# Shifting the SBUF buffers of a banded-attention and MoE kernel against each other by a few dozen bytes

## The chip, the cores and the metric

The kernel runs on one core of one Trainium2 chip. The metric is the device time of one execution in microseconds; the median of three runs of the kernel before is 660.24 us (659.09 to 661.42).

## The reference

Attention over 2 batches, 8 heads, 768 positions and 64 dimensions, in which each position sees its neighbours within 16 positions and, beside them, 24 summaries of blocks of 32 (the maximum of k, the mean of v). Two feed-forward stages follow on 1536 tokens of width 512:

```python
def _attn_ref(q, k, v):
    k_sum = k.reshape(B, H, nb, block, D).max(axis=3)
    v_sum = v.reshape(B, H, nb, block, D).mean(axis=3)
    scores_l = scale * np.matmul(q, k.transpose(0, 1, 3, 2))
    mask_l = np.abs(pos[:, None] - pos[None, :]) < window
    scores_s = scale * np.einsum('bhsd,bhnd->bhsn', q, k_sum) + np.log(block)
    a = softmax(concat([where(mask_l, scores_l, -1e9), scores_s]))
    return a @ concat([v, v_sum], axis=2)

def _moe_ref(x, w_a, w_b, w_out):        # 512 -> 1536 -> 512
    return ((x @ w_a) * (x @ w_b)) @ w_out

def _moe2_ref(x, w_in, w_out):           # 512 -> 2048 -> 512
    h = x @ w_in
    return (h - np.tanh(h)) @ w_out
```

## The kernel before

All matrices are held in float32. For the products of the two MoE stages each operand is split into a high and a low part of type fp32r, and three matmuls stand for one product: high by high, high by low, low by high. The tokens are handled in three blocks of 512, the hidden width in pieces of 128: 12 pieces in the first stage, 16 in the second.

The matmuls of these stages have 128 rows and columns of stationary weights and a moving operand of 512 columns, and stand on three lines:

- `proj` (line 370), called by `pos_a`, `pos_b` and `pos_h`: stationary a slice of the split weights `wsp`, moving a slice of the split tokens `X`, which lie in buffer `XA` or `XB`. Twelve matmuls make one PSUM tile (`pa`, `pb`, and in the second stage also `ps`, `pt`).
- `pos_o` (line 398): stationary `wsp`, moving `gh` or `gl`, the split gated hidden piece. Twelve matmuls, three into each of four `acc` tiles.
- `pos_o2` (line 459): stationary a slice of `gh` or `gl`, or, for every third piece, of two buffers of `vw`; moving the split weights `wsp`. Twelve matmuls into four `acc` tiles.

`wsp` has four buffers of 4096 bytes of each partition; one is filled for each piece of weights, by ACT (line 184, high part) and DVE or POOL (line 185, low part). Weights arrive as raw words by DMA in `stage`, `x21a` and `x21b` and are decoded by ACT, POOL and DVE into `w`.

The order of the work is a table: the list `pos` holds the steps of the two MoE stages, and a plan hangs the attention of the second batch (`T1`, `T2`, `T2b`, `T3`, `T4`) and the decoding of weights on its places, so that attention fills the first 300 us between the products of the first stage. The attention of the first batch stands ahead of it, as a list of operations by hand (`SEQ`). Attention's products are plain fp32: `T2m` (line 288; scores; moving `kw`, in steps of 480 bytes, stationary `qbd`, in steps of 512), transposes against `ident` (lines 223, 269, 327), `T4` (line 340), and the mean of v in `mean_v` (line 240; stationary `mavg` of 24 columns). A plain fp32 product has two records in the trace, an fp32r product or a transpose one.

Every buffer is a tile of one pool, `sb`, made by `st(shape, tag, bufs)`. The pool gives each tag its bytes in the order in which the tags are first asked for; the sizes that were asked for earlier decide where a later one lies. Nothing but such a size separates two neighbours. In the kernel before, one tile that nothing uses, `pad1` (128 bytes of each partition, line 780), follows `kt` (12672 bytes, 128 more than a multiple of 256).

Of the kernel before, what the change touches and what calls it, by code (L numbers as in the profile page):

```python
# [39 lines left out]
def band_attention_moe_kernel(ctx: ExitStack, tc: tile.TileContext, q, k, v, w_a, w_b, w_out, w_in, w_out2, out):  # L40
# [22 lines left out]
    def st(shape, tag, bufs=1, dt=F32):  # L63
        return sb.tile(shape, dt, tag=tag, bufs=bufs, name=tag)

    def pt(tag, shape=(128, 512)):
        return ps.tile(list(shape), F32, tag=tag, name=tag)
# [8 lines left out]
    qbd = st([128, 2, NP, 128], "qbd")  # L76
    qbd2 = st([128, 2, NP, 128], "wsp", 4)

    xb = st([128, 2 * KC * TB], "XB")
    kq = xb[:, 0:3072].rearrange("p (c h d) -> p c h d", c=NC, h=H)  # L80
    qbd4 = st([128, 2, NP, 128], "wsp", 4)
# [2 lines left out]
    def constants():  # L84
        nc.vector.memset(bsq, -math.sqrt(GA) * GB)
        nc.vector.memset(bth, -GC2)
        nc.vector.memset(qbd2, 0.0)
        nc.gpsimd.memset(qbd3, 0.0)

        for m, n, r in ((mavp, KW + 2 * NB - 8, BLK // 2), (mavg, 2 * NB - 4, BLK)):  # L90
            nc.gpsimd.memset(m, 1.0 / BLK)
            nc.gpsimd.affine_select(
                out=m, in_=m, pattern=[[-r, n]], compare_op=ALU.is_gt, fill=0.0,
                base=(n - NB) * r + 1, channel_multiplier=1,
            )
            nc.gpsimd.affine_select(
                out=m, in_=m, pattern=[[r, n]], compare_op=ALU.is_gt, fill=0.0,
                base=r - (n - NB) * r, channel_multiplier=-1,
            )
        nc.gpsimd.memset(qbd4, 0.0)  # L100
        for m, off in zip(masks, (0, WIN, 2 * WIN)):
            nc.gpsimd.memset(m[:, 0:KW], 0.0)
            nc.gpsimd.memset(m[:, KW:NK], math.log(BLK) / SC)
            for h in range(2):
                band = m[h * 64 : h * 64 + 64, 0:KW]
                nc.gpsimd.affine_select(
                    out=band, in_=band, pattern=[[1, KW]], compare_op=ALU.is_gt, fill=NEG,
                    base=WIN - off, channel_multiplier=-1,
                )
                nc.gpsimd.affine_select(  # L110
                    out=band, in_=band, pattern=[[-1, KW]], compare_op=ALU.is_gt, fill=NEG,
                    base=WIN + off, channel_multiplier=1,
                )
# [76 lines left out]
    kt, knat, qn, vst, qb, at_x, X = {}, {}, {}, {}, {}, {}, {}  # L190
    kwb = [st([128, NP, NK], "kw", 2) for _ in range(2)]
    kwb += [st([128, NP, NK], "w", 3 * F1) for _ in range(2)]
    vwb = [st([NK, H, D], "vw", 3) for _ in range(3)]
    vwx = [st([NK, H, D], "w", 3 * F1) for _ in range(5)]
    kwx = {}
    qx = {}
# [576 lines left out]
    with tc.manual_schedule():  # L773
        nc.vector.memset(qbd, 0.0)
        for _ in range(WARM):
            mm(pt("ps")[:, 0:256], qbd[:, 0, 0, :], qbd[:, 0, 0:2, :], start=True, stop=True)
        make_identity(nc, ident)
        XAv = st([128, 4, 2 * TB], "XA")
        kt[0] = st([128, NP, S + NB], "kt")
        st([128, 32], "pad1")  # L780
        constants()
        for n in SEQ.split():
            exec(compile(f"def op_{n}(op): op('{n}')\n", "<ops>", "exec"), globals())
            globals()["op_" + n](op)
# [50 lines left out]
```

## Time and profile before

| | kernel before |
|---|---|
| median of three runs | 660.24 us (659.09 to 661.42) |
| profiled execution, its own time | 659.97 us |
| span of its instructions | 658.2 us |
| mean granted TensorE clock | 0.995 |
| PE busy | 637.4 us, 97% of the span |
| DVE, ACT, POOL busy | 501.9, 475.1, 209.1 us |
| moved by DMA | 62.11 MB |

The profile lists for each engine its instructions with start and duration. PE is TensorE streaming the moving operand, PEld the loading of weights, which runs beside it. Matmuls are pipelined: a record lasts longer (389 ns) than the distance to the next one's start, so the distance is what counts. "128x512" is partitions by elements. `acc<-gh,wsp` names what is written and the two operands.

### The profile page before, as it was taken

The numbers are of one execution on the slowest core, as the hardware profiler recorded it, in microseconds if no ns is written. First come the engines' busy times: TensorE is split into PE (matmuls) and PEld (weight loads), VectorE is DVE, ScalarE is ACT, GpSimd is POOL, SyncE is SP. The second block draws the span as 40 slices with busy tenths as digits, with TensorE's granted clock in tenths as the row PEclk, the third lists the DMA queues.
The fourth block names the chain that finished last, engine by engine and source line by source line (L and its number), as shares of the span: only waits on it lengthen the run. The fifth ranks groups of instructions, "written<-read, shape, count | busy, mean of one in ns | idle before, by whom it ended". The sixth has DMA issues, their size and how long they took to land.

```text
span 658.2 us, 9626 instructions
## 1 busy us (share of the span) xinstructions
PE 637.4 (97%) x3240; PEld 518.2 (79%) x3240; DVE 501.9 (76%) x999; ACT 475.1 (72%) x1000; POOL 209.1 (32%) x221
## 2 busy tenths in 40 slices
PE   7779999999799999999999999999999999999997
PEld 5567876888588888888888888888888888888885
DVE  5889999898675777747877749777777877777775
ACT  4899886897686787645655548777777777777774
POOL 6752231222000011100111134554444554444441
PEclk9979999999999999999999999999999999999999
DMA  9996984563324554513444200000010000010001
GB/s 203 242 240 185 249 224 127 176 214 116 81 89 124 164 161 141 154 54 113 143 145 145 80 1 0 1 0 1 1 64 1 0 1 0 26 40 1 1 0 64
DMA packets 84781, 62.11 MB, mean 94 GB/s; under 512 B 51892, under 2 KB 75444, under 8 KB 84732
## 3 DMA queue, kind: packets, MB, share of 16 engines
q1 hardware_dynamic: 84732, 61.50, 33.3%
q8 instruction: 25, 0.41, 0.3%
q14 instruction: 24, 0.20, 0.1%
HBM read 54.00 MB, written 7.34 MB: 93 GB/s over the span
## 4 chain that ended last, share of the span: by engine, by line
PE 83%; DVE 8%; ACT 4%; DMA 2%; issue 2%; SPq 1%; POOL 0%; DVEq 0%; ACTq 0%
PE acc L459 20%; PE pb L370 18%; PE pa L370 17%; PE acc L398 12%; PE pt L370 5%; PE ps L370 5%; PE ps L288 1%; DVE w L164 1%; PE ps L340 1%; DVE wsp L185 1%; DMA stage<-in_moe_w_in_dram 1%; DVE w L165 1%; PE pt L240 1%; PE pt L327 1%; SPq L610 1%
## 5 line engine op out<-in xcount | busy, mean ns | idle before, releaser
L185 POOL TENSOR_TENSOR wsp<-w,wsp 128x512 fp32r<-128x512 f32 x97 | 127.4, 1330 | 140.0 <-ACT wsp L184 140.0
L184 ACT ACTIVATE wsp<-w 128x512 fp32r<-128x512 f32 x201 | 121.3, 622 | 17.8 <-PE acc L398 8.0
L185 DVE TENSOR_TENSOR wsp<-w,wsp 128x512 fp32r<-128x512 f32 x104 | 73.9, 712 | 41.0 <-ACT wsp L184 40.8
L179 POOL TENSOR_SCALAR w<-w 128x512 f32<-128x512 f32 x52 | 41.8, 809 | 181.7 <-ACT w L154 168.9
L398 PE MATMUL acc<-gh,wsp 128*128 128x512 f32 x288 | 96.5, 394 | 1.2 <-ACT gh L363 1.2
L370 PE MATMUL pa<-XA,wsp 128*128 128x512 f32 x336 | 85.2, 402 | 2.1 <-ACT XA L720 2.1
L370 PE MATMUL pb<-XA,wsp 128*128 128x512 f32 x336 | 83.9, 393 | 1.4 <-DVE tg L386 1.4
L459 PE MATMUL acc<-wsp,gh 128*128 128x512 f32 x256 | 78.8, 389 | 0.0
L370 PEld LDWEIGHTS pa<-XA,wsp 128*128 128x128 f32 x336 | 64.1, 193 | 16.6 <-ACT XA L720 2.4
L370 PEld LDWEIGHTS pb<-XA,wsp 128*128 128x128 f32 x336 | 62.1, 188 | 14.9 <-ACT x21a L155 1.7
L363 ACT ACTIVATE gh<-tg 128x512 fp32r<-128x512 f32 x68 | 42.4, 624 | 33.9 <-DVE tg L386 33.6
L398 PEld LDWEIGHTS acc<-gh,wsp 128*128 128x128 f32 x288 | 53.7, 188 | 11.9 <-ACT gh L363 1.3
L370 PE MATMUL pb<-XB,wsp 128*128 128x512 f32 x240 | 60.8, 396 | 0.0
L370 PE MATMUL pa<-XB,wsp 128*128 128x512 f32 x240 | 60.0, 394 | 0.0
L398 PE MATMUL acc<-gl,wsp 128*128 128x512 f32 x144 | 56.8, 396 | 1.1 <-DVE gl L364 1.1
L459 PEld LDWEIGHTS acc<-wsp,gh 128*128 128x128 f32 x256 | 48.1, 188 | 9.9
L364 DVE TENSOR_TENSOR gl<-tg,gh 128x512 fp32r<-128x512 f32 x68 | 46.8, 688 | 9.1 <-ACT gh L363 8.9
L370 PEld LDWEIGHTS pa<-XB,wsp 128*128 128x128 f32 x240 | 44.5, 188 | 9.4 <-DVE XB L348 0.2
L370 PEld LDWEIGHTS pb<-XB,wsp 128*128 128x128 f32 x240 | 44.4, 188 | 9.2
L459 PE MATMUL acc<-wsp,gl 128*128 128x512 f32 x128 | 49.8, 389 | 0.0
L459 PE MATMUL acc<-wsp,vw 128*128 128x512 f32 x192 | 46.5, 391 | 0.0
L459 PEld LDWEIGHTS acc<-wsp,vw 128*128 128x128 f32 x192 | 35.9, 188 | 8.2 <-ACT vw L363 0.4
(304 smaller groups left out, 1175.5 us busy)
## 6 DMA issues: line engine op xcount, KB each, us to landing
stage<-in_moe_w_out_dram SPq DMA_DIRECT2D x19, 512.0 KB, 3.5
stage<-in_moe_w_in_dram SPq DMA_DIRECT2D x16, 512.0 KB, 5.6
stage<-in_moe_w_a_dram SPq DMA_DIRECT2D x8, 512.0 KB, 5.0
w<-wsc SPq DMA_DIRECT2D x16, 256.0 KB, 3.4
vw<-in_v_dram SPq DMA_DIRECT2D x19, 192.0 KB, 3.0
stage<-in_moe_w_b_dram SPq DMA_DIRECT2D x7, 512.0 KB, 5.6
wsc<-x21a SPq DMA_DIRECT2D x8, 256.0 KB, 5.1
wsc<-x21b SPq DMA_DIRECT2D x8, 256.0 KB, 4.9
```

Of the source, the lines that this page charges most:

```text
L164: nc.vector.scalar_tensor_tensor(r, t[:, :, 1], -0x40000000, r, op0=ALU.bitwise_and, op1=ALU.bitwise_or)
L165: nc.vector.tensor_tensor(r, r, t[:, :, 0], op=ALU.add)
L179: nc.gpsimd.tensor_scalar(rf, rf, HI_HI, HI_LO, op0=ALU.min, op1=ALU.max)
L184: nc.scalar.activation(s[:, 0, :], r, AF.Copy)
L185: eng.tensor_tensor(s[:, 1, :], r, s[:, 0, :].bitcast(F32), op=ALU.subtract)
L240: mm(pp, mavg[:, NB - 4 - 4 * c : 2 * NB - 4 - 4 * c], vch.pop(c).rearrange("p h d -> p (h d)"), start=(c == 0), stop=(c == NC - 1),)
L288: mm(pp[:, p, 0:NK], qt[:, p, :], kw[:, p, :], start=True, stop=True)
L363: nc.scalar.activation(dst[0], src, AF.Copy)
L364: eng.tensor_tensor(dst[1], src, dst[0].bitcast(F32), op=ALU.subtract)
L370: mm(dst, w, xx, start=(kk == 0 and n == 0), stop=(kk == KC - 1 and n == 2))
L398: mm(acc[blk][d][:, c0:c1], w, t, start=(f == 0 and c0 == 0 and n == 0), stop=(f == F1 - 1 and n == 2))
L459: mm(a[c], g[:, cs], s[:, i, :], start=(f == 0 and n == 0), stop=(f == F2 - 1 and n == 2))
```

## The change

Three tiles are made that nothing uses, and a fourth grows. They add 64, 32, 224 and 224 bytes to each partition, and every tile that is first asked for behind one of them moves up. No instruction, wait or transfer is added, left out or moved: on PE, DVE, ACT, POOL and SP the instructions stand in the same order with the same waits as before.

```diff
--- before.py
+++ after.py
@@ -76,6 +76,7 @@
     qbd = st([128, 2, NP, 128], "qbd")
     qbd2 = st([128, 2, NP, 128], "wsp", 4)
 
+    st([128, 16], "pada")
     xb = st([128, 2 * KC * TB], "XB")
     kq = xb[:, 0:3072].rearrange("p (c h d) -> p c h d", c=NC, h=H)
     qbd4 = st([128, 2, NP, 128], "wsp", 4)
@@ -190,7 +191,9 @@
     kt, knat, qn, vst, qb, at_x, X = {}, {}, {}, {}, {}, {}, {}
     kwb = [st([128, NP, NK], "kw", 2) for _ in range(2)]
     kwb += [st([128, NP, NK], "w", 3 * F1) for _ in range(2)]
+    st([128, 8], "padb")
     vwb = [st([NK, H, D], "vw", 3) for _ in range(3)]
+    st([128, 56], "padc")
     vwx = [st([NK, H, D], "w", 3 * F1) for _ in range(5)]
     kwx = {}
     qx = {}
@@ -777,7 +780,7 @@
         make_identity(nc, ident)
         XAv = st([128, 4, 2 * TB], "XA")
         kt[0] = st([128, NP, S + NB], "kt")
-        st([128, 32], "pad1")
+        st([128, 32 + 56], "pad1")
         constants()
         for n in SEQ.split():
             exec(compile(f"def op_{n}(op): op('{n}')\n", "<ops>", "exec"), globals())
```

Start addresses of the buffers that matter, in bytes of a partition, modulo 256 (buffers of one tag are a multiple of 256 apart):

| tag | first address before | modulo 256 | first address after | modulo 256 |
|---|---|---|---|---|
| wsp, qbd, qn | 28960 (wsp) | 32 | 28960 | 32 |
| XB | 45344 | 32 | 45408 | 96 |
| kw, w | 61728 (kw) | 32 | 61792 | 96 |
| vw | 139552 | 32 | 139648 | 128 |
| XA | 145696 | 32 | 146016 | 96 |
| kt | 162080 | 32 | 162400 | 96 |
| x20a, x20b, stage, x21a, x21b, e, ta, tg, at | 174880 (x20a) | 32 | 175424 | 64 |
| gh | 216096 | 32 | 216640 | 64 |
| gl | 220192 | 32 | 220736 | 64 |

The slices that the matmuls of lines 370, 398 and 459 take begin at multiples of 256 bytes within their buffers. Moving less stationary address, modulo 256, is therefore 0 for all of them before, and after: 64 on line 370, 32 on line 398, -32 on line 459 with `gh` or `gl` as weights, and -96 there with `vw`.

## Rows read from the trace of the kernel before

**Rows 1.** The page: span, and busy us of each engine with its share of the span.
```profile
span 658.2 us, 9626 instructions
...
PE 637.4 (97%) x3240; PEld 518.2 (79%) x3240; DVE 501.9 (76%) x999; ACT 475.1 (72%) x1000; POOL 209.1 (32%) x221
```

**Rows 2.** The page: the chain that ended last, by engine, then by line.
```profile
PE 83%; DVE 8%; ACT 4%; DMA 2%; issue 2%; SPq 1%; POOL 0%; DVEq 0%; ACTq 0%
PE acc L459 20%; PE pb L370 18%; PE pa L370 17%; PE acc L398 12%; PE pt L370 5%; PE ps L370 5%; PE ps L288 1%; DVE w L164 1%; PE ps L340 1%; DVE wsp L185 1%; DMA stage<-in_moe_w_in_dram 1%; DVE w L165 1%; PE pt L240 1%; PE pt L327 1%; SPq L610 1%
```

**Rows 3.** The chain in order of time (start us, us, what), three quiet stretches.
```profile
289.25 2.72 PE acc L398 x12
291.97 2.72 PE pa L370 x12
...
422.53 2.72 PE acc L459 x12
425.25 2.72 PE pt L370 x12
...
645.57 5.44 PE acc L459 x24
```

**Rows 4.** By stretch: us, busy us of PE, PEld, DVE, ACT, POOL; clock, DMA share, GB/s.
```profile
60.00:120.00 60.00, 60.00 (x327) 46.18 (x326) 55.73 (x121) 49.03 (x109) 14.67 (x18) 1.00 0.76 200
300.00:360.00 60.00, 60.00 (x266) 49.74 (x265) 47.70 (x75) 36.02 (x65) 7.57 (x11) 1.00 0.42 147
480.00:540.00 60.00, 60.00 (x266) 49.71 (x265) 47.59 (x74) 46.98 (x84) 29.85 (x22) 1.00 0.05 18
```

**Rows 5.** By stretch, the whole span: line 370, then 398, then 459; last, 459 with vw.
```profile
0.00:658.30 658.30, 353.46 (x1440) 268.94 (x1440) 0.99 0.34 94
...
0.00:658.30 658.30, 109.50 (x432) 79.81 (x432) 0.99 0.34 94
...
0.00:658.30 658.30, 138.59 (x576) 108.03 (x576) 0.99 0.34 94
...
L459 PE MATMUL acc<-wsp,vw 128*128 128x512 f32 x192 | 46.5, 391 | 0.0
```

**Rows 6.** PE in order of time (start us, us, line, operation), after attention work.
```profile
231.66 0.39 PE L398 MATMUL acc<-gl,wsp 128*128 128x512 f32 x1
231.89 0.62 PE L398 MATMUL acc<-gh,wsp 128*128 128x512 f32 x2
232.36 0.40 PE L398 MATMUL acc<-gl,wsp 128*128 128x512 f32 x1
232.59 0.62 PE L398 MATMUL acc<-gh,wsp 128*128 128x512 f32 x2
233.05 0.39 PE L398 MATMUL acc<-gl,wsp 128*128 128x512 f32 x1
```

**Rows 7.** The chain in order of time, groups of twelve after attention work.
```profile
94.69 2.77 PE pa L370 x12
...
226.83 2.75 PE pb L370 x12
```

**Rows 8.** Line 370: min/median/max ns of its records, first and last start.
```profile
L370 PE MATMUL pb<-XB,wsp x240: 387/390/499, 177.6 to 634.3; 128*128 128x512 f32 x120
...
L370 PE MATMUL ps<-XB,wsp x96: 389/389/390, 397.9 to 639.7; 128*128 128x512 f32 x96
```

**Rows 9.** The chain in order of time, attention products and transposes.
```profile
254.86 0.44 PE pt L327 x4
...
256.23 0.89 PE ps L288 x8
```

**Rows 10.** PE in order of time, line 240.
```profile
99.12 1.88 PE L240 MATMUL pt<-x20b,mavg 128*24 128x512 f32 x4
100.84 1.88 PE L240 MATMUL pt<-w,mavg 128*24 128x512 f32 x4
```

**Rows 11.** The chain in order of time, the head.
```profile
6.26 5.13 DMA x20a<-in_q_dram
```

## The prediction

> **What bounds the kernel now.** I read the page's shares first, then the chain of waits, then stretches, then single matmuls. PE is busy for 637.4 of 658.2 us [rows 1], and the chain that ends last runs over PE for 83% of the span, nearly all of it on three lines: the two projections (line 370), the product with w_out (398) and the last product (459) [rows 2]. From about 300 us on PE never waits: each group of twelve matmuls of 128x512 follows the one before after 2.72 us, whatever line and operands it has (acc of line 398, pa, pt, acc of line 459), and twenty-four after 5.44 [rows 3]. That is 226.7 ns from one start to the next, at a granted clock of 1.00 [rows 4], the 2.4 GHz level. There are 1440 such matmuls on line 370, 432 on line 398 and 576 on line 459, 192 of the last with vw [rows 5]; 2448 of them at 226.7 ns make 554.9 us, 84% of the span. So the time is this one price, and little else: 1 ns more or less per matmul is 2.4 us, 0.37% of the time. What a measurement of this kernel tells from no change is about 0.3%, or 2 us.
>
> **What the change removes, adds and moves.** It adds no instruction, wait or transfer and moves none in the order. What moves are addresses: X (XA, XB) by 64 bytes against the split weights wsp, gh and gl by 32, vw by 96. The sum has therefore four terms, all a count times an unknown difference: 1440 matmuls of line 370 (moving operand 64 bytes ahead of the stationary one), 432 of line 398 (32 ahead), 576 - 192 = 384 of line 459 with gh and gl as weights (32 behind), 192 with vw (96 behind).
>
> *Is the pitch one that an address can touch?* Two things speak for it. After an interruption by attention work, matmuls of the same shape start 470 and 460 ns after the last but one (starts 231.89 to 232.36 and 232.59 to 233.05, 235 and 230 ns each) [rows 6], where two at 226.7 are 453; groups of twelve then take 2.74 to 2.77 us, up to 230.8 ns each [rows 7]. No wait lies between them, and nothing in these instructions differs from the later ones, so the price of a matmul has a part that depends on how its reads fall in time, and it settles at 226.7. The records themselves say the same: those of pb<-XB, which lie in both parts, begin at 387 ns with a median of 390 and run longer, those of ps<-XB, which lie after 397 us alone, all take 389 to 390 [rows 8]. A stream whose reads meet the weight load's reads would look like this.
>
> Four things speak against an effect. First, the addresses of the pairs in rows 3 differ in their higher bits (wsp, XB, vw, XA, gh and gl lie between 29 and 224 KB of a partition), and all take 2.72 us: only the part below 256 bytes is untried. Second, the score products of line 288 are a trial of that part on a smaller scale: their moving operand kw steps by 480 bytes and their weights by 512, so the four products of a unit lie 0, -32, -64 and -96 bytes apart, and eight records (two for each) take 0.89 us, 110 ns each [rows 9]; the transposes of line 327, at 96, 128, 160 and 192 apart, take 0.44 us for four, 110 ns again. Their loads of 128 columns set that pitch, so a stall of the moving stream is hidden there: it shows that the load doesn't depend on the offset, not that the stream doesn't. Third, the two reads don't keep their distance: by rows 9 a load of 128 columns (512 bytes of a partition) takes 110 ns, and by rows 3 the stream of 512 columns (2048 bytes) 227 ns. While the weights' 512 bytes pass, the stream passes 2048 x 110/227 = 990, so the distance between them sweeps some 480 bytes, close to two full turns of 256, whatever it was at the start. If meetings cost time, each start offset then meets about as often. Fourth, the stream finds its own phase: after the interruption of rows 6 and 7 a later group is back at 2.72 us [rows 3], so an offset may only move the phase at which it settles.
>
> On ports the Trainium skill ("TensorE: Matmul & The Clock Gate", Part 2, step 1) says that TensorE reads the streaming operand and the weights through two independent ports, so that loading the next weights takes no bandwidth from the running matmul; by that the sum is zero. The unsteady pitch of rows 6, with nothing waiting, is hard to fit to it, so the rule alone does not settle the question.
>
> *Bounds of the price.* Below: the plain fp32 products of line 240 have two records for each product, with weights of 24 columns, and four start in 1.72 us, 430 ns each [rows 10]; if such a pass streams its 512 columns at half the rate of an fp32r pass, a pass without loss is 215 ns, 11.7 ns under rows 3. For all 2448 that is -28.6 us. Above: the unsettled pitch of 230.8 ns for good [rows 7], +4.1 ns or +10.0 us; the worst single step of rows 6, 235 ns, would be +20 us. Between 215 and 235 I take **no difference**, 226.7 ns, because it is the row that is nearest in kind: the same instructions, in the settled state, over every pair of buffers.
>
> *What else the addresses touch.* DVE, ACT and POOL read and write moved buffers; they lie beside PE (in the quiet stretches 47.7 and 36.0 of 60 us, later 47.6 and 47.0 [rows 4]) and cost nothing unless they grow by a quarter; between 60 and 120 us, where DVE is busy for 55.7 of 60 us, 1% of it would be 0.6 us. The loads of the head land at other places of the same buffers: the one on the chain there, of q, takes 5.13 us [rows 11]; I take zero and bound it by a tenth of that, 0.5 us either way. The unused pieces themselves cost space, no time.
>
> **Sum.** 659.97 us of the profiled execution (span 658.2 and 1.8 around it) plus 0 from four terms plus 0 for the rest is 660.0 us. The median of the runs shown is 660.24, 0.3 us above that execution, inside the spread of those runs.
>
> **Rivals.** *Faster: the settled pitch holds a collision of equal offsets, and the change takes it out.* For it: 226.7 stands 11.7 ns over the 215 of rows 10, and both operands start at the same place below 256 bytes in every one of the 2448. Against it: the sweep above. Not all of the gap need go, nor at each of the four offsets. Half the gap on all, 5.85 ns, is -14.3 us: 645.7; the whole gap on line 370 alone, 1440 x 11.7 = -16.8 us: 643.1; the whole on all: 631.4, and less than that in truth, since between 60 and 120 us DVE at 55.7 of 60 would begin to bound. I give 645 as this case's time. The skill's back-to-back gap of a warm matmul (same page, "Back-to-back issue gap": N/2.4 + 2.5 ns) gives 215.8 ns for 512 columns, an estimate; the settled 226.7 of rows 3 stands 10.9 ns over it. By that rule this case would end at 659.97 - 2448 x 10.9 ns = 633.3 us, though the page doesn't say that an address is what the rest is paid for.
>
> *Slower: equal offsets are the good case.* With equal offsets the stream settles at 226.7, under the 230 and 235 of rows 6; at another offset it may settle higher or not at all, and keep the unsettled 230.8 of rows 7. The place is any of the four terms; the price is +4.1 ns each: 670.0 us if all do, 665.9 if only line 370 does, 664.1 if only lines 398 and 459 do. It decides from the first product on, and shows as twelve matmuls in 2.77 us where 2.72 stood. For it: what is seen of other phases in rows 6 and 7 costs more than the settled one. Against it: it settles again after each interruption, whatever phase that leaves.
>
> *The change does not do what it says:* the offsets follow from the order in which buffers are first asked for, and the allotted addresses do stand 64, 32, -32 and -96 apart; I give this nothing.
>
> **How the numbers follow.** No difference 0.42, faster 0.32, slower 0.26. The likeliest is 660.0 us, with a range of its own of 658.5 to 661.5 (the spread of the runs shown). For 8 in 10 the range must reach into both others: down to 643, which takes in half the gap on all and the whole gap on line 370, and leaves out the whole gap (0.06); up to 671, which takes in 230.8 ns for good, and leaves out what is dearer (0.12).
>
> **What will show it.** Right: groups of twelve in 2.72 us on all three lines, and span within 2 us of 658.2. Each term shows by itself: pa, pb, ps and pt groups for +64, acc of line 398 for +32, acc of line 459 with gh or gl as weights for -32 and with vw for -96. A group at 2.58 us (215 ns) makes the first rival right, one at 2.77 the second. The forecast is wrong if any of the 1440 leaves 2.72 us; it is wrong in another way if the groups hold 2.72 and the span still moves, for then the cost lies ahead of 300 us, in PE's idle time.

## The result: 1.4% slower, paid on all three lines of the MoE stages

| | before | changed |
|---|---|---|
| median | 660.41 us (4 runs, 659.09 to 661.42) | 669.18 us (4 runs, 668.83 to 670.03) |
| ratio, with its 95% interval | | 1.0136 (1.0115 to 1.0156) |
| profiled execution, its own time | 659.97 us | 670.03 us |
| span | 658.2 us | 668.3 us |
| PE busy | 637.4 us | 647.3 us |
| DVE, ACT busy | 501.9, 475.1 us | 502.9, 475.5 us |

The time lies inside the stated range and on the side of the second rival. The page of the changed kernel has the added time on PE; the other engines' busy times are those of before [rows 1]:

```profile
span 668.3 us, 9626 instructions
...
PE 647.3 (97%) x3240; PEld 519.4 (78%) x3240; DVE 502.9 (75%) x999; ACT 475.5 (71%) x1000; POOL 208.8 (31%) x221
```

The chain of the changed kernel in order of time (start us, us, what), two quiet stretches. Line 373 is line 370 of before, 401 is 398, 462 is 459:

```profile
299.97 2.79 PE acc L401 x12
302.76 2.75 PE pa L373 x12
305.51 2.75 PE pb L373 x12
...
410.50 2.80 PE acc L462 x12
413.30 2.75 PE pa L373 x12
416.05 2.81 PE acc L462 x12
418.86 2.80 PE pb L373 x12
```

In these stretches every group of twelve, which took 2.72 us before [rows 3], takes 2.75 to 2.81, with nothing waiting in between. Below, the distance of a product is the start address of its moving operand less that of its stationary one, modulo 256 bytes; its price is the time from one start to the next; and a group has settled when its price no longer changes. The group of line 462 at 416.05 has vw as weights, the one at 410.50 gh and gl. Divided by twelve, the prices are 229.2 ns at distance 64, 232.5 at 32, 233.3 at -32, 234.2 at -96, against 226.7. With the counts of [rows 5] the four terms are 1440 x 2.5 = 3.6, 432 x 5.8 = 2.5, 384 x 6.7 = 2.6 and 192 x 7.5 = 1.4 us, 10.1 in all. That is somewhat too much, since groups amid attention stood at up to 2.77 before [rows 7] and stand at 2.75 to 2.77 now, and somewhat too little for the groups of X that follow vw (418.86, 2.80 us). Averaged over all matmuls of a line whose next one starts within 300 ns, attention aside, the two traces differ by 2.5, 4.9, 6.8 and 7.6 ns, 9.8 us in all. The medians differ by 8.8 us.

The records of one group show where the time was added (min/median/max ns, first and last start):

```profile
L373 PE MATMUL pb<-XB,wsp x240: 387/393/502, 179.2 to 644.1; 128*128 128x512 f32 x120
...
L373 PE MATMUL ps<-XB,wsp x96: 388/393/398, 402.0 to 649.6; 128*128 128x512 f32 x96
```

Records of ps<-XB, all 389 to 390 before [rows 8], now run from 388 to 398: the price varies from matmul to matmul. From the first of them to the last it is 247.6 us now and was 241.8 before (397.9 to 639.7), 5.8 us more; 4.1 us were lost ahead of it, and 0.2 behind. Of the 4.1 us, 0.9 lie before the first matmul of pa<-XA (at 43.4 us, 42.5 before); the other kernels below start it at 42.3 to 42.6, so this is likely the profiled execution's own, which is also the slowest of the four.

### The profile page after: what moved, and what is told of

The parts are those of the page before. It is cut to its first block, busy times and chain, and to the rows that moved or that the text cites. A ratio compares the mean times of both kernels' runs of the same rounds, so it can differ in the third digit from the quotient of the medians.

```text
span 668.3 us, 9626 instructions
## 1 busy us (share of the span) xinstructions
PE 647.3 (97%) x3240; PEld 519.4 (78%) x3240; DVE 502.9 (75%) x999; ACT 475.5 (71%) x1000; POOL 208.8 (31%) x221
## 4 chain that ended last, share of the span: by engine, by line
PE 88%; DVE 4%; ACT 3%; DMA 2%; issue 1%; SPq 1%; POOL 0%; DVEq 0%; POOLq 0%; ACTq 0%
PE acc L462 20%; PE pb L373 19%; PE pa L373 18%; PE acc L401 14%; PE pt L373 5%; PE ps L373 5%; PE ps L291 2%; PE ps L343 1%; DMA stage<-in_moe_w_in_dram 1%; PE pt L330 1%; PE pt L243 1%; SPq L613 1%; DMA x20a<-in_q_dram 1%; DVE w L165 1%; DVE w L166 1%
## 5 line engine op out<-in xcount | busy, mean ns | idle before, releaser
L180 POOL TENSOR_SCALAR w<-w 128x512 f32<-128x512 f32 x52 | 40.4, 781 | 186.3 <-ACT w L155 186.2
L462 PE MATMUL acc<-wsp,gh 128*128 128x512 f32 x256 | 80.6, 396 | 0.0
L462 PE MATMUL acc<-wsp,vw 128*128 128x512 f32 x192 | 47.9, 398 | 0.0
```

The lines of the kernel that those rows point to most:

```text
L180: nc.gpsimd.tensor_scalar(rf, rf, HI_HI, HI_LO, op0=ALU.min, op1=ALU.max)
L462: mm(a[c], g[:, cs], s[:, i, :], start=(f == 0 and n == 0), stop=(f == F2 - 1 and n == 2))
```

## The experiments

### Which distance costs what: matmuls alone

The three stages are left out; one loop runs fp32r matmuls between two buffers, and each group has its own PSUM name. Offsets in this code count words of 4 bytes (three lines are cut at "..."):

```diff
+    def group(name, d, s=0, cols=128, width=512, plain=False, reps=36):
+        n[0] += 1
+        p = ps.tile([128, 512], F32, tag="b%d" % (n[0] % 8), name=name)
+        for i in range(reps):
+            w0 = s + 128 * (i % 7)
+            m0 = s + d + 512 * (i % 3)
+            w, m = wt[:, w0 : w0 + cols], mv[:, m0 : m0 + width]
...
+            nc.tensor.matmul(p[0:cols, 0:width], w, m, start=(i == 0), stop=(i == reps - 1))
...
```

> This kernel leaves out attention and both MoE stages: it only runs groups of 36 fp32r matmuls of 128x512 between one buffer of weights and one of moving data, each group at another distance of the two (daa to dap: 0 to 240 bytes in steps of 16; dba and on: 256 to 480 in steps of 32; fine: 4, 8, 12), then with both moved together (both: 16, 32, 64, 128 bytes, distance 0), with fewer weight columns (colz at distance 0, cold at 64: 32, 64, 96 columns), with 256 moving columns (half), and as plain fp32 (plain). A record's mean less some 162 ns is the distance between starts. Theory A, the distance of the two operands decides through meetings of the two reads: distance 0 has 389 ns; 64, 32, 224 and 160 have about 391, 395, 396 and 398, as the changed kernel has; groups moved together have 389; and with 32 weight columns a quarter of the stall is left, so that a group comes nearer to 377 (215 ns between starts). Theory B, the place of each operand for itself decides: the groups moved together leave 389 too. Theory C, the 13 ns over 213 belong to the change of weights whatever the reads do: fewer weight columns change nothing, and distance 0 stays at 389.

The chain of this kernel, groups of 36 (start us, us, what). daa is distance 0, dac 32, dae 64, dak 160, dao 224, dap 240, dba 256; botha and bothb: both operands 16 and 32 bytes further; colza 32 columns of weights; plain: plain fp32 at distance 0 and 64, 18 products in 36 records:

```profile
26.44 8.16 PE daa L53 x36
...
42.93 8.40 PE dac L53 x36
...
59.73 8.25 PE dae L53 x36
...
109.78 8.43 PE dak L53 x36
...
143.44 8.40 PE dao L53 x36
151.84 8.17 PE dap L53 x36
160.00 8.20 PE dba L53 x36
...
252.11 8.39 PE botha L53 x36
260.50 8.21 PE bothb L53 x36
...
285.09 8.32 PE colza L53 x36
...
343.53 15.45 PE plainz L53 x36
358.98 15.45 PE plaind L53 x36
```

With neither attention nor DMA nor another engine beside it, distance 0 has 8.16/36 = 226.7 ns, and 64, 32, 224 and 160 have 229.2, 233.3, 233.3 and 234.2: within 0.8 ns the four prices of the changed kernel. 256 is back near 0, so the pattern does repeat after 256 bytes; 8.20 against 8.16 is the settling at the group's start. Theory A holds for moves of both operands by 32 bytes, but not by 16: botha, at distance 0, has 233.1. And A's mechanism falls as far as it went by the amount read: with a quarter of the weight columns the group is dearer, 231.1 ns, not near 215. Nor is C right, since the distance matters. Fewer bytes of weights do not lower the price.

### Moving everything together

```diff
+    st([128, 16], "pad0")
     ident = st([128, 128], "ident")
```

> One unused piece of 64 bytes ahead of every buffer: all operands move, none against another. Theory A (the distance of the operands decides): 660.4 us, groups of twelve in 2.72 us. Theory B (each operand's own place modulo 256 decides): the groups leave 2.72 us and the time moves by 2 to 10 us.

Measured 659.63 us against 660.64, ratio 0.9992 (0.9979 to 1.0004). The chain:

```profile
422.10 2.72 PE acc L460 x12
424.82 2.72 PE pt L371 x12
```

So it is the distance between the operands, not the place of each, as far as moves of 64 bytes go.

### Each half of the change

```diff
+    st([128, 16], "pada")
     xb = st([128, 2 * KC * TB], "XB")
...
+    st([128, 48], "padb")
...
+    st([128, 16], "padc")
...
-        st([128, 32], "pad1")
+        st([128, 16], "pad1")
```

> Only XA and XB lie 64 bytes from wsp, gh, gl and vw at 0. Theory A: line 370 at some 229.1 ns as in the changed kernel, 1440 x 2.4 ns = +3.5 us, 663.9 us; lines 398 and 459 back at 226.7. If the price came from other engines or the loads of the head, the sum would not split by line and this would stand near 660 or near 669.

Measured 666.51 us, ratio 1.0097 (1.0077 to 1.0117): 2.6 us more than expected. The chain shows why:

```profile
419.68 2.77 PE acc L462 x12
422.44 2.76 PE ps L373 x12
```

X takes 2.76 us, near its term. But line 462 (459 of before), whose operands lie at distance 0 here, takes 2.77 and not 2.72.

```diff
+    st([128, 24], "padb")
...
+    st([128, 40], "padc")
...
-        st([128, 32], "pad1")
+        st([128, 40], "pad1")
```

> Only gh and gl (32 bytes from wsp) and vw (96) are moved, X at 0. Theory A: line 370 at 226.7, 398 and 459 at the changed kernel's 232 to 237 ns, 432 x 5.8 + 576 x 7 ns = +6.5 us, 666.9 us; together with the kernel that moves X alone this makes the whole of the change. Otherwise as for that kernel.

Measured 667.02 us, ratio 1.0105 (1.0084 to 1.0126). Both halves cost, on their own lines:

```profile
295.77 2.72 PE pb L372 x12
298.49 2.80 PE acc L400 x12
301.29 2.76 PE pa L372 x12
304.05 2.72 PE pb L372 x12
```

The first group of X behind a group of line 400 (398 of before) takes 2.76 us, the second 2.72: the disturbed phase is carried over and dies out within twelve matmuls or so. That the total came near the 666.9 us expected is in part luck, since nothing for X was in that sum. The expected split failed on this: the halves lose 5.9 and 6.4 us against 660.64, 12.3 together where the change loses 8.8, because each half alone also raises the price of groups that lie at distance 0 in it.

### The grid, and what the price hangs on

```diff
+        for i in range(16):
+            for j in range(16):
+                p = group("w" + AZ[i] + "m" + AZ[j], 4 * (j - i), s=4 * i, reps=24)
```

> Leaves out attention and both MoE stages. 256 groups of 24 matmuls of 128x512: weights at 0, 16, ... 240 bytes past a multiple of 256 (plus 128), moving data likewise, every pair. If only the distance counts, the grid is constant along its diagonals: settled at 226.7 ns between starts (record 389 to 390) for distances 0 and 240, 229 to 235 elsewhere. The group with both at 16 bytes in the first map (233 ns at distance 0) speaks against that: if the place of each within 32 bytes counts too, the diagonal of distance 0 is at 226.7 for even steps of 16 and near 233 for odd ones. A cell under 226 ns would give a kernel that is faster than the one before; I expect none, since a settled start falls on multiples of 6.67 ns and 220 was never seen.

Mean distance of starts in the last twelve matmuls of each group, in ns, by the distance of the operands and by whether the weights start at an even or an odd multiple of 16 bytes. The eight rows of a kind agree within 0.8 ns except where two values stand:

```
distance    0     16    32    48    64    80    96    112
even      226.7 231.7 233.3 233.3 228.9 231.1 233.3 231.1
odd       230.0 228.3 232.2 232.0 226.7 230.0 233.3 226.7
          /233.3 /226.7      /230.0
distance  128    144   160   176   192   208   224   240
even      232.5 233.3 234.2 233.3 233.3 234.5 233.3 226.7/233.3
odd       233.3 233.3 226.7 231.8 228.9 233.3 226.7 226.7/233.3
          (one even cell at 176 has 231.1)
```

The chain of this kernel shows cells with the weights at 0 and at 16 bytes (w: weights, m: moving, a to p: 0 to 240 bytes); 24 matmuls at 226.7 ns take 5.44 us:

```profile
27.60 5.44 PE wama L53 x24
...
55.30 5.54 PE wamf L53 x24
...
122.25 5.59 PE wbmb L53 x24
...
144.46 5.45 PE wbmf L53 x24
```

The tiles of this pool start at multiples of 32 bytes, so the kernels live in the even rows. There 0 is the cheapest distance; 240 equals it in seven cells of eight, and stands at 233.3 in the other. The changed kernel's 64, 32, 224 and 160 have 228.9, 233.3, 233.3 and 234.2. At odd places distance 0 has 230.0 in seven cells and the 233 that was expected in one. No cell of the 256 lies under 226.6 ns. The most common values are 226.7 and 233.3, which are 34 and 35 times 6.67 ns; 228.9, 231.1 and 234.2 are not, so the reason given for expecting no lower cell holds only in part.

The next kernel has the loop of the first map with these two lines changed:

```diff
-            w0 = s + 128 * (i % 7)
-            m0 = s + d + 512 * (i % 3)
+            w0 = s + 128 * (0 if one else i % 7) + ws * (i % 2)
+            m0 = s + d + 512 * (0 if one else i % 3) + ms * (i % 2)
```

> Leaves out attention and both MoE stages. Steps of 4 bytes (faa to fdp, 24 matmuls each); widths of 64 to 512 columns at distance 0 (widz) and 32 (widd); weights in turn at two places 64 bytes apart (altw), moving data in turn at two such places (altm); one and the same pair of slices again and again (onez at distance 0, oned at 64); twelve matmuls at distance 64 in turn with twelve at 0 (seqd, seqz), and at 240 with 0 (seqn, seqm). Theory D, a matmul pays at its start for a phase in which both reads find their place, whatever its length: at each width the distance between starts is the columns at 2.4 GHz plus 10 to 20 ns, and the groups at distance 0 that stand between groups at 64 do not settle within twelve, so seqz has about 231 ns, as lines 398 and 459 had when X alone was moved. Theory E, the price is paid along the stream (the reads meet again and again): the excess grows with the columns, and is a quarter at 128; seqz is at 226.7, as any group at distance 0.

The chain, groups of 36 at distance 0 (widz) with 256, 320, 384, 448 and 512 columns, the same at distance 32 (widd; granted clock 1.00 in both stretches), then twelve at 64 in turn with twelve at 0, then twelve at 240 with twelve at 0:

```profile
402.41 4.33 PE widzd L53 x36
406.73 5.28 PE widze L53 x36
412.02 6.24 PE widzf L53 x36
418.26 7.43 PE widzg L53 x36
425.69 8.21 PE widzh L53 x36
...
452.45 4.23 PE widdd L53 x36
456.68 5.28 PE widde L53 x36
461.95 6.24 PE widdf L53 x36
468.19 7.43 PE widdg L53 x36
475.62 8.40 PE widdh L53 x36
...
533.67 2.76 PE seqd L53 x12
536.43 2.77 PE seqz L53 x12
...
561.29 2.80 PE seqn L53 x12
564.10 2.72 PE seqm L53 x12
```

At distance 0 these are 13.6, 13.3, 13.3, 19.7 and 14.7 ns over the columns at 2.4 GHz (106.7, 133.3, 160.0, 186.7 and 213.3 ns), the last with its settling. So the excess at distance 0 does not grow with the columns, as theory D has it, and E is wrong.

What a distance of 32 adds is another matter, and neither theory has it. It is 0.19 us for 36 matmuls at 512 columns, nothing at 320, 384 and 448, and at 256 columns distance 32 is the cheaper one by 0.10 us (in the first map 36 matmuls of 256 columns took 4.30 us at distance 0 and 4.24 at 64). The surcharge is thus neither a fixed price of each matmul nor one that grows along the stream; it was seen at 512 columns, the width of the kernel's matmuls.

seqz has 230.8 ns though its own distance is 0, which is the surplus of the half with X alone. Steps of 4 bytes gave up to 240 ns, and nothing under 226.6. With the weights in turn at two places 64 bytes apart (altw, distances 0 and 192) 36 matmuls took 8.28 us, between the two prices; with the moving data so (altm, distances 0 and 64) they took 8.33 us, more than at either alone.

### Two forecasts from the grid

```diff
-        st([128, 32], "pad1")
```

> The unused piece pad1 of the kernel before is taken away: gh and gl lie 128 bytes from wsp, X and vw at 0. By the grid (232.5 ns at distance 128 with weights at an even step) lines 398 and, with gh or gl, 459 leave 226.7 by 5.8 ns: 816 x 5.8 = +4.7 us. The phase that they leave behind costs the groups of X between them another 1.2 ns as in the kernel with gh and vw moved, 1440 x 1.2 = +1.7 us: some 666.5 us. If the change's loss had come from something else than these distances, no offset at 128 need cost anything: 660.

Measured 665.83 us against 659.68, ratio 1.0091 (1.0070 to 1.0113), 0.7 us less than expected. The chain:

```profile
300.37 2.79 PE acc L398 x12
303.17 2.73 PE pa L370 x12
305.90 2.72 PE pb L370 x12
```

2.79 us are 232.5 ns, as the grid says. So the unused piece that the kernel before already had is worth 0.9% of its time.

```diff
+    def shifted(tag):
+        t = st([128, 2 * KC * TB + 64], tag, 1, F32R)
+        return t[:, 60 : 60 + 2 * KC * TB].rearrange("p (i k t) -> p i k t", i=2, k=KC)
...
-        X[i] = st([128, 2, KC, TB], xtag[i % 2], 1, F32R)
+        X[i] = shifted(xtag[i % 2])
...
-            xs[blk] = st([128, 2, KC, TB], xtag[(blk + 1) % 2], 1, F32R)
+            xs[blk] = shifted(xtag[(blk + 1) % 2])
```

> X is a slice that starts 240 bytes into its buffer, which is 16 bytes before equal modulo 256; gh, gl and vw at 0. In the maps this distance has two settled states: 226.7 ns when entered from some phases, 233.3 when twelve of it follow twelve at distance 0 (seqn), and then the twelve at 0 keep 226.7. In the kernel groups of twelve do follow groups at 0, so line 370 should stand at 233.3: 1440 x 6.7 = +9.6 us, 670.0 us, with lines 398 and 459 at 226.7. If the state is chosen otherwise in the kernel, all stand at 226.7, and it is 660 or, by shorter settling after attention, up to 1 us less.

Measured 668.36 us against 659.68, ratio 1.0139 (1.0110 to 1.0168): 8.7 us lost where 9.6 were expected.

```profile
302.06 2.80 PE pa L374 x12
304.86 2.80 PE pb L374 x12
307.66 2.72 PE acc L402 x12
```

Distance 240 stands in its dear state here, at 233.3 ns, in the order in which the kernel alternates; the groups at distance 0 keep 226.7. A cell of the grid alone does not tell the price where two states exist.

No version beats the kernel before: its operands lie at the lowest price that was found. Groups amid attention still take up to 2.77 us where settled ones take 2.72 [rows 3, 7]; a layout that settles sooner was not tried.

## Why the prediction was wrong, point by point

- **What bounds the kernel** was right: PE's pitch on three lines, 1 ns of it 2.4 us. DVE, ACT and POOL had no part: their busy times moved by 1.0 us at most.
- **The step that failed** is the choice within the bounds: "Between 215 and 235 I take no difference, 226.7 ns, because it is the row that is nearest in kind". The rows said that the price hangs on a phase [rows 6, 7] and that one pair of places settles at 226.7 [rows 3]; that every other pair would settle there too was not in them. All four terms of the sum were put at nothing; measured in their place were 229.2, 232.5, 233.3 and 234.2 ns, that is +2.5, +5.8, +6.7 and +7.5 ns for each matmul.
- Two of the four arguments behind it were unsound. The third, the sweep ("each start offset then meets about as often"), supposed that the reads meet all along the stream, so that the start offset averages out. At 512 columns it does not: 233.3 ns at distance 32 against 226.7 at 0. 32 weight columns in place of 128 don't lower the price either. At 320 to 448 columns the two distances do cost the same; why 512 differs is not shown. The fourth, "an offset may only move the phase at which it settles", is contradicted by the maps: most offsets settle at a higher price, or at a pattern of several. The first was true (higher address bits don't matter: the price is the same at 0 and 256), and the second, the attention products, was weighed rightly as no evidence: matmuls of 64 columns, whose stream is far shorter, took 109 ns as well (3.94 us for 36 in the kernel with the widths), which bears out that the 110 ns of [rows 9] are not set by the stream. The transposes show the same with 120 weight columns, not the 128 that the prediction gives.
- **The rival "slower: equal offsets are the good case"** had the mechanism, and its reason (what is seen of other phases costs more) was the reading to follow. Its size was off: it priced every term at +4.1 ns; they are 2.5, 5.8, 6.7 and 7.5 ns. That its total, 670.0, came out near 669.18 is luck: the largest term has the smallest price, so the mean of the four is again 4.1 ns.
- **The rival "faster"**, with its 215 ns of [rows 10], fell. The 430 ns of a plain fp32 pass hold at distances 0 and 64 alike (plainz and plaind of the first map, 36 records in 15.45 us each), so that form does not show the effect, and half of its pass, 215 ns, was reached by no fp32r group of 512 columns. The gap of N/2.4 + 2.5 ns that the Trainium skill gives for a warm matmul by itself ("TensorE: Matmul & The Clock Gate", Back-to-back issue gap) was not reached by fp32r at any offset or at 256 to 512 columns either; at 512 columns 226.7 ns is the lowest, 10.9 over the estimate of 215.8. The independent read ports of the Trainium skill (same page, Part 2, step 1) may stand as far as bandwidth goes, since fewer weight columns gain nothing; that no relation of the two addresses matters, as the prediction drew from them, is refuted here at 512 columns.

Shown, for fp32r matmuls of 512 columns: the price follows the distance modulo 256 and the weights' place within 32 bytes, also with no other engine at work, and a group's place changes the price of the group that follows. Not shown: by what mechanism. Every matmul of these kernels loads its weights, so no run tells whether the price belongs to a meeting of the two reads; what has the period of 6.67 ns, and why a distance of 32 costs nothing at 320 to 448 columns, stay open too.

## What to carry to other kernels

Where fp32r matmuls of 512 columns bound a kernel, look at the operands' addresses modulo 256, weights against moving data: here, with weights at multiples of 32 bytes, equal ones cost 226.7 ns for each matmul and others up to 234.5 (at 16-byte steps), 3.4%. Don't carry this to other widths unmeasured: at 256 columns equal addresses were not the cheapest. Any buffer whose size is not a multiple of 256 bytes shifts all that is asked for behind it, so an unrelated resize can cost 1%; compare the time of twelve matmuls in a quiet stretch before and after. And when a trace shows that the same instruction has several prices by phase, take that as a reason to expect a price for anything that sets the phase.

## What was not expected of the hardware

- At distance 0 the excess over the columns' time does not grow with them: 13.3 ns at 320 and 384 columns, 13.3 at 512 once settled, 19.7 at 448.
- A distance of 32 bytes cost 6.7 ns at 512 columns and nothing at 320, 384 and 448; at 256 it was the cheaper place, 4.23 us for 36 against 4.33.
- Groups of one and the same kind have two settled states at a distance of 240 bytes (226.7 and 233.3 ns). Behind groups of twelve at distance 0 they took the dear one, in the loop and in the kernel; what chooses it is not shown.
- Both operands 16 bytes further at an unchanged distance of 0 cost 233.1 ns, 32 bytes further 226.7 once settled.
- Fewer weight columns made matmuls dearer at distance 0: 8.32 us for 36 with 32 columns, 8.16 with 128.
